# A new hand-laid order for a fused attention and feed-forward kernel: loads, transposes and stores placed anew, batch 2 transposed by DMA, scores by head group

## The chip, the cores and the metric

The kernel runs on one core of a Trainium2 chip. The metric is the time of one execution in microseconds (us). Three executions of the kernel before gave 248.44, 250.93 and 252.87; their median, 250.93 us, is the time before. A further execution was profiled; it took 247.08 us. A change of about 2% is told from no change.

## The reference

The inputs are q, k and v (8 batches, 8 heads, 576 rows, 64 columns) and two weight matrices (512 by 2048 and 2048 by 512). Per batch and head, attention is approximated with 32 landmarks (means of 18 rows):

```
q_lm, k_lm = means of 18 neighbouring rows of q and k          # 32 landmarks
A  = softmax(q    @ k_lm.T / 8)        # 576 x 32
Bm = softmax(q_lm @ k_lm.T / 8)        # 32 x 32
C  = softmax(q_lm @ k.T    / 8)        # 32 x 576
Z  = Bm.T / (norm1(Bm) * norminf(Bm) + 1e-6)
six times:  Z = 2 * Z - Z @ Bm @ Z
x   = A @ Z @ C @ v, heads side by side: 4608 rows of 512
h   = x @ w_in;  out = (h * sigmoid(h)) @ w_out
```

## The kernel before

**Tiling.** The work runs batch by batch. The 8 heads of a batch are two groups (g = 0, 1) of four heads, each with 32 landmarks, so that 128 partitions hold one group's landmarks. q and k arrive with the landmark block on the partitions (`qk`) and are turned into `qT`, with the head's columns on the partitions. `qk`, `qT` and v have two buffers, used by even and odd batches.

**Two ways to transpose.** For batches under `NTR` (3 before) TensorE transposes q and k by an identity (`tr`, 36 matmuls a batch, L515), and VectorE or ScalarE copies the result out of PSUM (`trc`). For later batches SP issues DMA transposes (`xt`, L539), four a batch: q and k by two groups. In the names `xt10.4` is k (1), group 0, batch 4. The exponentials of C (`ce`) have to be transposed too: by TensorE in batches 0 and 1 (`ctm`, `ctc`), by DMA later (`ct0`, `ct1`, L814).

**Per batch.** `ld1`, `ld0` load k and q, `ldv0` to `ldv2` v. `lra` to `lrd` add up the landmarks on VectorE as a tree (L575); in batches 0 and 1 TensorE does it (`lms`). `ltr`, `lmT` transpose the sums; `sb`, `pb` and the names up to `nsd` are Bm and the six steps for Z, which go back and forth between TensorE and VectorE. `A` and `C` are the scores, `Ax`, `Cx` their exponentials on ScalarE; `S`, `Ln`, `Rs`, `etn` normalise A; `cv` multiplies the transposed C with v; `zt`, then `m` multiplies Z C v into `w_in` (copies `mc`).

**Feed-forward.** `h0` to `h15` and `hx0`, `hx8` multiply the normalised A with `m`; `g`, `gx` apply the activation (ScalarE). `p1` to `p7` are seven half-size products of a Strassen-like scheme for 256 rows (names end in `@5000` plus 100 times the batch plus 0, 20 or 40); `ss` are its sums on VectorE, `c1` to `c22` and `u2` copies and additions from PSUM into `ost` (six buffers). `o0` to `o3` is the plain product for the first 256 rows. Each `os` is four stores of 64 KB from SP (in the last batch single ones from SP and ScalarE).

**What sets the order.** `SEQUENCE` lists all steps by name; each engine executes its own in this order, and a queue (SP's, POOL's) issues its DMAs in it. `*n` are n matmuls on zeros that fill TensorE's time. After a slash stands the engine where there is a choice. The list also sets which PSUM bank a step gets. Dependencies in the step objects (`deps`) are asserted against the list; those that concern data become waits, others were rules for the planner that made the list. One kind becomes waits of its own (`o.after`): a transpose `xt` or `ct` waits for the second v load, as it stands in the program, and a load waits for a transpose, so that the two kinds of transfer alternate:

```
            gate = v_ops[b][-2:-1]                    # before an xt of batch b
        gate = last[b - 1].get("xts", [])[-2:-1]      # before the loads of batch b
        if b - 2 >= NCT:
            gate = gate + last[b - 2]["cts"][:1]
```

The order of the two in `xts` is that of the program (k group 0, k group 1, q group 0, q group 1), not that of the list. ScalarE has two sets of tables, for exp/ln and for the activation; each change between them is a table load.

## Time and profile before

| | |
|---|---|
| profiled execution | 247.08 us, its span 245.4 us, granted clock 0.985 in the mean |
| runs of the kernel | 248.44, 250.93, 252.87 us |
| TensorE busy | 233.3 us, 2948 matmuls |
| VectorE, ScalarE busy | 180.0 us, 180.8 us |
| DMA queues | loads (POOL) 18.06 MB; SP's queue 17.35 MB |
| transposes of q and k by DMA | 20, issue to landing 4.2 us in the median |
| transposes of `ce` by DMA | 12, 3.9 us |
| table loads on ScalarE | 12, 1.28 us each |

The page gives busy time by engine, then the span in 40 slices: each digit is a busy share in tenths, and PEclk the clock that TensorE was granted. A windows line has, for a stretch, its length, the busy time of TensorE, its weight loads, VectorE, ScalarE and POOL (instructions in brackets), the granted clock, the DMA share and GB/s. A line of the waits says who waited for whom, the total, the number and the longest. In the chain of work that ended last, the first number is the start and the second the duration.

### The profile page before, as it was taken

The page shows a single profiled execution, that of the slowest core. Times are in us where ns is not written, and L with a number is a line of the kernel's source. Part 1 is how long each engine was busy: PE and PEld are TensorE (multiplying, and loading weights), DVE is VectorE, ACT ScalarE, POOL GpSimd, SP SyncE. Part 2 cuts the span into 40 slices and gives each one's busy share as a digit, 9 for nine tenths or more (in the row PEclk, how much of TensorE's full clock was granted, in tenths as well). Part 3 has the DMA queues.
Part 4 walks back from the last instruction along what each step waited for, and adds up shares of the span by engine and source line. Part 5 has one row for each costly group of instructions (what it writes and reads, how often), then busy time and mean ns, then how long its engine had stood idle before and what let it go on. Part 6 is the DMA issues. An engine that isn't in the chain of part 4 may idle for free.

```text
span 245.4 us, 7471 instructions
## 1 busy us (share of the span) xinstructions
PE 233.3 (95%) x2948; PEld 165.8 (68%) x2948; DVE 180.0 (73%) x503; ACT 180.8 (74%) x432; POOL 36.7 (15%) x62
## 2 busy tenths in 40 slices
PE   7999999999999999199999999999999999999992
PEld 5986464457867556067878754777876765789882
DVE  2589889789998591489798968938899475348752
ACT  3299999988989998159746699999779788634100
POOL 8346713000050040000130060000000000000000
PEclk9999999999999999769999999999999999999999
DMA  6999999999999999793999999985414421012343
GB/s 160 207 203 197 206 207 206 210 205 204 132 177 220 202 137 178 185 194 98 136 190 171 167 185 239 190 145 136 108 47 117 121 52 39 1 43 77 88 119 109
DMA packets 55876, 36.84 MB, mean 150 GB/s; under 512 B 36640, under 2 KB 47392, under 8 KB 55840
## 3 DMA queue, kind: packets, MB, share of 16 engines
q0 software_dynamic: 15120, 18.06, 45.1%
q1 hardware_dynamic: 39808, 17.35, 34.9%
q10 hardware_dynamic: 912, 0.95, 1.4%
q8 instruction: 23, 0.38, 0.6%
q14 instruction: 13, 0.11, 0.1%
HBM read 36.70 MB, written 9.44 MB: 188 GB/s over the span
## 4 chain that ended last, share of the span: by engine, by line
PE 78%; ACT 7%; DMA 7%; SPq 3%; issue 1%; DVE 1%; ACTq 0%; DVEq 0%
PE ps L325 74%; DMA qT<-qk 6%; PE ps L515 3%; SPq L539 2%; ACT gm L913 2%; DMA gm<-in_k_dram 1%; ACT L913 1%; SPq L814 1%; ACT L1116 1%; ACT gx L936 1%; ACT m L335 1%; PE ps L802 1%; DVE red L575 1%; ACT pb L641 1%; ACT et L742 0%
## 5 line engine op out<-in xcount | busy, mean ns | idle before, releaser
L913 ACT ACTIVATE gm<-ps 128x512 f16<-128x512 f32 x128 | 68.7, 621 | 15.0 <-PE ps L325 14.3
L325 PE MATMUL ps<-etn,m 128*128 128x512 bf16 (+1 forms) x512 | 73.5, 289 | 0.2
L325 PEld LDWEIGHTS <-gm 128*128 128x128 f16 x512 | 48.6, 98 | 12.5 <-issue 1.3
L325 PE MATMUL ps<-w_out_sb,gm 128*128 128x256 f16 (+1 forms) x392 | 53.0, 281 | 0.0
L325 PEld LDWEIGHTS <-ss 128*128 128x128 f16 x408 | 39.5, 99 | 9.8 <-issue 1.8
L325 PEld LDWEIGHTS <-m 128*128 128x128 bf16 x512 | 31.5, 98 | 20.8 <-issue 3.2
L325 PE MATMUL ps<-wt,ss 128*128 128x256 f16 x272 | 35.5, 276 | 0.2
L1036 DVE TENSOR_TENSOR ost<-ost,ps 128x256 f32<-128x256 f32 x51 | 20.9, 416 | 13.4 <-PE ps L325 7.4
L335 ACT COPY ost<-ps 128x256 f32<-128x256 f32 (+1 forms) x45 | 17.2, 388 | 10.9 <-PE ps L325 10.6
L335 ACT CAST m<-ps 128x512 bf16<-128x512 f32 x36 | 19.4, 612 | 1.1 <-PE ps L325 0.8
L337 DVE CAST m<-ps 128x512 bf16<-128x512 f32 x28 | 18.3, 685 | 2.3 <-PE ps L325 1.9
L710 DVE SCALAR_TENSOR_TENSOR st<-st,ps 128x128 bf16<-128x128 bf16 (+2 forms) x54 | 13.6, 257 | 8.5 <-PE ps L325 5.5
L407 POOL DMA_DIRECT2D v<-in_v_dram x24 | 14.0, 590 | 30.8 <-DMA qT<-qk 13.6
L325 PE MATMUL ps<-w_out_sb,ss 128*128 128x256 f16 x136 | 17.5, 273 | 0.0
L325 PE MATMUL ps<-wt,gm 128*128 128x256 f16 x120 | 15.5, 272 | 0.0
L575 DVE TENSOR_TENSOR red<-qT 128x1024 f16<-128x1024 bf16 x12 | 8.3, 689 | 9.4 <-DMA qT<-qk 9.2
L685 DVE TENSOR_TENSOR fb<-st,hmask 128x256 bf16<-128x256 bf16 (+1 forms) x54 | 14.4, 271 | 0.8
L752 ACT ACTIVATE ln<-ps 128x288 f32<-128x288 f32 x32 | 12.4, 423 | 2.7 <-PE ps L325 2.4
L787 ACT ACTIVATE ce<-ps 128x288 bf16<-128x288 f32 x32 | 13.0, 424 | 1.7 <-PE ps L325 1.6
L1001 DVE TENSOR_TENSOR ss<-gm 128x1024 f16<-128x1024 f16 x15 | 10.2, 686 | 5.2 <-ACT gm L913 5.2
L742 ACT ACTIVATE et<-ps 128x288 bf16<-128x288 f32 x32 | 11.1, 423 | 3.6 <-PE ps L325 3.6
L337 DVE COPY ost<-ps 128x256 f32<-128x256 f32 x25 | 10.5, 420 | 3.2 <-PE ps L325 3.0
(93 smaller groups left out, 332.0 us busy)
## 6 DMA issues: line engine op xcount, KB each, us to landing
out_dram<-ost SPq DMA_DIRECT2D x126, 64.0 KB, 2.1
v<-in_v_dram POOLq DMA_DIRECT2D x24, 192.0 KB, 10.0
qk<-in_q_dram POOLq DMA_DIRECT2D x7, 576.0 KB, 10.6
qk<-in_k_dram POOLq DMA_DIRECT2D x7, 576.0 KB, 9.2
w_out_sb<-in_moe_w_out_dram POOLq DMA_DIRECT2D x4, 512.0 KB, 15.1
w_in_sb<-in_moe_w_in_dram POOLq DMA_DIRECT2D x8, 128.0 KB, 7.2
w_in_sb<-in_moe_w_in_dram POOLq DMA_DIRECT2D x4, 256.0 KB, 9.0
out_dram<-ost ACTq DMA_DIRECT2D x10, 64.0 KB, 1.7
```

The source lines that it names most:

```text
L325: nc.tensor.matmul(out=out_ap, lhsT=lhsT, rhs=rhs, start=start, stop=stop, skip_group_check=True)
L335: nc.scalar.copy(out=out, in_=in_)
L337: nc.vector.tensor_copy(out=out, in_=in_)
L407: lambda e, a=a: nc.gpsimd.dma_start(out=v_r[b % 2][a * L:(a + 1) * L, :, :], in_=v[b].rearrange("h (l a x) d -> a l h (x d)", l=L, a=VA)[ ...
L575: lambda e: nc.vector.tensor_tensor(out=o_, in0=a_, in1=b_, op=OP.add),
L685: nc.vector.tensor_tensor(out=fb[it % 2][:, g0:g1], in0=bc(sr[it % 3][:, g0:g1, 0:L], 4, 2), in1=bc(hmask, n, 1), op=OP.mult), [o], 14.5 + ...
L710: nc.vector.scalar_tensor_tensor(out=s2[:, g0:g1, lo:SW], in0=s[:, g0:g1, lo:SW], scalar=2.0, in1=ps[:, 0:NG * SW].rearrange("p (g x) -> p ...
L742: lambda e, g=g, et=et, c=c: nc.scalar.activation(out=et[:, c], in_=bank(me["A"], 2 * g + c)[:, 0:HS], func=AF.Exp, scale=sc / J),
L752: lambda e, g=g, c=c, ln=ln: nc.scalar.activation(out=ln[:, c], in_=bank(me["S", g, c])[:, 0:HS], func=AF.Ln),
L787: nc.scalar.activation(out=ce[:, :, 0:VP].rearrange("p (i c) (a l) -> p c a i l", c=2, a=VA)[:, c], in_=bank(me["C"], 2 * g + c)[:, 0:HS]. ...
L913: lambda e, dc=dc, cell=cell: nc.scalar.activation(out=gm[:, dc, :], in_=bank(cell["o"]), func=AF.Silu),
L1036: nc.vector.tensor_tensor(out=out_, in0=x, in1=y, op=OP.add)
```

## The change

- `SEQUENCE` is laid out anew from first step to last: other places on every engine, other engines for some copies (the copies `c` are 33 on ScalarE for 31, `mc` 40 for 36), 67 filler matmuls for 64, 14 table loads for 12.
- `NTR` is 2: batch 2 is transposed by DMA; 36 matmuls and 8 copies go, four DMA transposes come.
- The two groups of k, and of q, are one step (`xt1`, `xt0`), issued one behind the other; the step that others wait for is the first of its two transposes. k always comes first, so the loads of the next batch wait for the first half of q.
- `A` and `C` are two steps each, one by head group, with two PSUM banks a step for four at once.
- Rules of the planner alone go: eight loads in flight at most (`swdge`), A and C after the landmarks' exponentials, the first activation after batch 1's exponentials, most sums of `w_out` after the plain product.

The code, cut:

```diff
-    NTR = 3
+    NTR = 2
...
-        d = list(deps) + list(after)
-        if len(swdge) >= 8:
-            d.append((swdge[-8], None))
+        d = list(deps) + [(x, 0.8) if x.name[:2] == "xt" else x for x in after]
...
-                dep = [a] + plain
+                dep = [a] + (plain if i == 2 else [])
...
-                for g in range(NG):
-                    qt_ops[t, g] = [A(
-                        f"xt{t}{g}.{b}", [("SP", 1.38)],
-                        lambda e, t=t, g=g: nc.sync.dma_start_transpose(
-                            out=qT[:, t, g], in_=qk[:, t, g].rearrange("p j d -> p (j d)")),
-                        [qk_ops[b, t, g]] + use + gate, p0 + 5, lag=XLAG)]
-                    qt_ops[t, g][0].after = gate
-                    me["qk_read"] += qt_ops[t, g]
-                    me["xts"] += qt_ops[t, g]
+                o = A(f"xt{t}.{b}", [("SP", 2.76)],
+                      lambda e, t=t: [nc.sync.dma_start_transpose(
+                          out=qT[:, t, g], in_=qk[:, t, g].rearrange("p j d -> p (j d)"))
+                          for g in range(NG)][0],
+                      [qk_ops[b, t, g] for g in range(NG)] + use + gate, p0 + 5, lag=XLAG)
+                o.after = gate
+                qt_ops[t, 0] = qt_ops[t, 1] = [o]
+                me["qk_read"].append(o)
+                me["xts"] = [o]
...
-        def am(e):
-            for g in range(NG):
+        for g in range(NG):
+            def am(e, g=g):
...
-        me["A"] = A(f"A.{b}", [("PE", 0.26)], am,
-                    lmT_all + ([] if cr else [(pb_op, -0.2)]) + qt_ops[0, 0] + qt_ops[0, 1] + ready, p0 + 20,
-                    psum=4, tiled="q")
+            me["A", g] = A(f"A{g}.{b}", [("PE", 0.142)], am,
+                           lmT_all + qt_ops[0, g], p0 + 20,
+                           psum=2, tiled="q")
...
-        gate = last[b - 1].get("xts", [])[-2:-1]
+        gate = last[b - 1].get("xts", [])
```

The order of the list around the transposes that the prediction speaks of, before (batch 4's transposes, batch 5's loads) and after:

```diff
-nsd40.3 ct0.3 xt00.4 ld1.5 ldv0.4 h9.2 g9.2 g14.2 h1.2 h0.2 g1.2 g0.2 cv0.3 ldv1.5 fb50.3
-ss30@5120.0 ns50.3 wc.3 nsd50.3 zbd.3 ld0.5 h11.2 g11.2 h13.2 g4.2 g13.2 h3.2 g3.2 etn1.3 zt.3
...
-g11.3 p1@5200.0 g3.3 h8.3 g8.3 ss00@5200.0 p5@5200.0 hx0.3 g14.3 g9.3 ss00@5220.0 xt11.4 xt01.4
-xt10.4 ss10@5200.0 lra1.4 lrb1.4 lrc1.4 ss10@5220.0 ss20@5220.0 lrd1.4 lra0.4 lrb0.4 os@5020.0
-ss20@5200.0 l1done.2 ltr1.4 h1.3 h0.3 g0.3 g1.3 g12.3 h15.3 gx0.3 c1@5200.0/DVE p6@5200.0
...
+sb.3 p1@5220.0 l1done.2 gx0.2 ss00@5220.0 gx8.2 xt1.4 C0.3 ss00@5200.0 A1.3 pb.3 p5@5220.0
+ss10@5220.0 ss10@5200.0 p4@5120.0 ss20@5220.0 Cx01.3 p1@5200.0 c1@5220.0/ACT pbs.3 xt0.4 Ax11.3
...
+ct0.3 lra1.4 c5@5220.0/ACT ns00.3 S10.3 p7@5220.0 Ax00.3 Ln10.3 nsd00.3 Cx10.3 fb10.3 os@5021.0
+lrb1.4 S01.3 ns10.3 S00.3 p3@5220.0 Ln01.3 nsd10.3 lrc1.4 Ln00.3 fb20.3 c22@5220.0 Rs0.3 ns20.3
+p5@5200.0 nsd20.3 lrd1.4 ct1.3 ld1.5 fb30.3 lra0.4 ltr1.4 S11.3 ns30.3 p4@5220.0 lmT1.4/ACT ld0.5
...
+fb50.3 cv0.3 wrc.3 Ax11.4 ss30@5200.0 p2@5200.0 Cx01.4 ldv0.5 wc.3 Ax10.4 Cx00.4 ldv1.5 etn0.3
...
+g1.4 ns00.5 h8.4 xt0.6 g10.4 nsd00.5 p2@5300.0 fb10.5 g14.4 ss20@5340.0 g2.4 h15.4 c1@5340.0/DVE
+g8.4 ns10.5 h13.4 nsd10.5 h5.4 fb20.5 g13.4 ss30@5340.0 p6@5340.0 ct1.5 g15.4 lra1.6 h11.4 ld1.7
```

For batches 0 to 2 the loads stand in the new list in this order from the weights on: `wi` pieces and batch 0's v, batch 1's v, `wo0` to `wo2`, `ld1.2`, `ld0.2`, `ldv0.2`, `ldv1.2`, `wo3`, `ldv2.2`; those of batch 3 come after batch 2's transposes on SP and, in SP's queue, eight stores (`os@5000`, `os@5001`), `xt1.3`, `ct0.2`, `ct1.2`, `xt0.3` follow.

## Prediction

> **What bounds the kernel now.** I read the first two parts of the page, then the windows around the one hole in TensorE's row, then who waited for whom, then the queues that feed it.

> ```profile
> span 245.4 us, 7471 instructions
> PE 233.3 (95%) x2948; PEld 165.8 (68%) x2948; DVE 180.0 (73%) x503; ACT 180.8 (74%) x432; POOL 36.7 (15%) x62
> PE   7999999999999999199999999999999999999992
> ...
> PEclk9999999999999999769999999999999999999999
> DMA  6999999999999999793999999985414421012343
> ```

> TensorE is the bound, with one hole, in slice 17. The same stretch in windows, the wait, and the chain:

> ```profile
> 95.00:100.00 5.00, 3.75 (x40) 2.66 (x37) 0.00 (x0) 4.19 (x9) 0.00 (x0) 1.00 1.18 200
> 100.00:105.00 5.00, 0.83 (x3) 0.43 (x4) 3.63 (x8) 0.00 (x0) 0.00 (x0) 0.65 0.70 180
> 105.00:110.00 5.00, 5.00 (x27) 3.11 (x26) 3.95 (x11) 2.75 (x7) 0.00 (x0) 0.66 1.03 197
> ```
> ```profile
> PE ps L325 <- DVE rs L575: 5.4, 1, 5.4
> ```
> ```profile
> 86.72 14.41 DMA qT<-qk
> ...
> 101.23 0.70 DVE red L575
> ```

> TensorE stands 5.4 us for the landmark sums of batch 4 (`ltr1.4`); VectorE could not add because half of k's transpose (`xt10.4`, issued 86.72) took 14.4 us. Then the granted clock is 0.65 and 0.66 in two windows: half speed from 101.5 to 108.4. Work resumed at 104.2, so 4.2 us at half speed lose 2.1 us more. The hole costs 7.5 us. Why 14.4:

> ```profile
> 86.34 0.71 POOL L400 DMA_DIRECT2D qk<-in_k_dram  x1 [13.68 <-issue]
> 87.04 1.16 POOL L407 DMA_DIRECT2D v<-in_v_dram  x2
> 88.20 0.71 POOL L400 DMA_DIRECT2D qk<-in_q_dram  x1
> ```
> ```profile
> DMA to landing us min/median/max: 3.3/4.2/14.4
> ```
> ```profile
> DMA to landing us min/median/max: 2.5/3.9/8.1
> ```

> (The last two: transposes of q and k; of `ce`.) The loads of batch 5 wait for one transpose, `xt00.4`, which stood first; the other three were still to come. In the trace's DMA packets (256 bytes are a transpose's, 768 to 2304 a load's) these loads run from 88.2 to 100.5, and `xt10.4`'s 1152 packets, 1.45 us when alone, run from 89.2 to 100.6: about 100 a us, 41 a us beside 2304-byte packets. `ct0.5` did the same (issued 129.3, first packet 133.4, when the 2304-byte load before it had landed). So: **a transpose that meets a load stream lands with its end.**

> To compare orders I lay TensorE's steps end to end at their undisturbed pitch (start to next start, 20th percentile by kind: `h` 0.43, `p` 0.87, `hx` 0.47, `A` or `C` 0.37, four or five transposes 0.22 or 0.28, filler 0.11). Before has 219.5 us of such work. The real start of a step minus its place in this sum is the delay so far: 4.0 at `sb.0`, 7.5 at `sb.2`, 9.4 just before the hole, 17.0 after it, 21.2 at the end.

> **The change, part by part.** The sum is made against the profiled execution's 247.08 us, its span and 1.68 around it; the median of the runs shown, 250.93, is 1.56% above, and the sum is scaled by that at the end. About 2% is what a measurement of this kernel can tell from no change.

> 1. TensorE loses batch 2's 36 transposes (nine take 0.50 us in the chain): -2.0. Three more fillers: +0.3. **-1.7**.
> 2. A and C in halves: the same 256 matmuls, each half 0.185 by the 0.37 of the whole. **0**; if each of 16 more borders cost 0.1, +1.6.
> 3. The hole: both halves of k and then of q now go out in one order, and the next loads wait for q's first half (and for a `ct` of two batches back). q's second half is issued 1.4 us behind; a load's first packet comes 1.4 to 2.4 us after its issue, so it is gone by then. **-7.5**.
> 4. VectorE loses batch 2's copies out of PSUM (7 at 0.42 to 0.49, about 3.2 us, near 37 us) and gets its tree of sums 9 us later. VectorE is 4.2 to 4.8 busy of 5 there, and the delay grows from 4.0 to 7.5 between 12 and 45 us. **-1.0**; between 0 and -3.4.
> 5. ScalarE has 14 table loads for 12, 1.28 us each; it is 74% busy and steps between holes. **0**; up to +2.6 if both land ahead of a waited-for copy.
> 6. Batch 2's transposes on SP. Up to `ldv2.2` the queue now loads 9.2 MB; before it moved 10.6 MB from 3.7 to 57.8 us (0.196 MB/us), so `ldv1.2`, for which `xt1.2` waits, lands near 47, and the rest (`wo3`, `ldv2.2`) at 50.8. Then four transposes at 1.45: last at 56, sums done at 57.7. `ltr0.2` stands at 50.1 of work, with the delay of 7.5 at 57.6. Nearly hidden, as are `o3` and `wt01`, which need `wo3`: **+0.5** (0 to 2). Queued behind on SP are eight stores of `os@5000` and `os@5001`; six `ost` buffers cover them.
> 7. Batch 3's loads now wait for batch 2's transposes: issue 54, first packet 56, then 1.57 MB with 0.52 MB of stores at 0.22 MB/us (205 to 241 GB/s in the windows from 70 to 80): `xt1.3` at 65.5. `ct0.2` and `ct1.2` are queued behind it, 2.8 and 1.25 us of issue, then 2.5: 72. TensorE is at `cv0.2` at 62.9 + 7.7 = 70.6, and `p4@5100` and all after it wait. **+1.4** (0 to 2.5).
> 8. Batch 4's loads, 1.57 MB and 1.05 MB of stores, end near 87.7; `xt1.4`'s second half lands near 92, 1.5 late for `lra1.4`, some of it covered before `ltr1.4`. **+1.0** (0 to 2.5).
> 9. The new meeting. On SP stand `ct0.3`, four stores, `ct1.3`. `ld1.5` waits for `ct0.3` only. Count from `ct0.3`'s issue: its landing at 2.5, `ld1.5` issued, first packet near 4.5 (4.0 to 5.0); SP issues 1.3 for `ct0.3`, 1.9 for the stores, 1.2 for `ct1.3`: first packet at 4.5 as well, and it needs 0.9 more. `ld1.5` and `ld0.5` are 1.18 MB, 6.0 us at 0.196; the v loads behind them wait for `cv0.3` itself. So `ct1.3` lands at 11.0. Between `ct0.3` and `cv0.3` TensorE has 6.7 us of work (6 `p`, 5 `ns`, 4 `S`, halves of A and C, three small ones). It stands 4.3 us, with no independent step behind. Like the first hole it then loses half of some 4 us: **+4.3 + 2.0**. Bounds: nothing, if the loads' first packet comes at 5.4 or later; 7.5 + 2.5, if the stream is as slow as 1.57 MB in 12.2 us was beside `xt10.4`.
> 10. `ct1.5` goes out just behind `xt0.6`, whose first half lets `ld1.7` go: its packets run from 4.3 to 5.2 us after `xt0.6`'s issue, the loads' from 4.7 to 5.7. **+0.5**.
> 11. The end: as before a last product, a copy and stores in two queues (4.4 us after the last matmul). **0**.

> On the 2.0 of step 9: the trace has one case, half clock from 2.8 us after TensorE stopped. [...]

> Sum: -1.7 - 7.5 - 1.0 + 0.5 + 1.4 + 1.0 + 6.3 + 0.5 = **-0.5**: 246.6 us, and 250.4 by the median. One hole goes and another comes.

> **The rivals.**

> *`ct1.3` escapes.* If the queues shared evenly, 0.9 us of packets would take 1.8 and land near 6.9, when TensorE is there anyway; so too if the loads start 0.9 us later. The sum loses 6.3: 240.3, or **244.0**. For it: starts of loads vary by 1 us, and `ct1.4` of before, 1.8 us ahead of a load's issue, landed in 3.8. Against: `xt10.4` at 41 packets a us, `ct0.5` at none. [...]

> *Both meetings cost, at the slow stream's price: slower.* The place is `ct1.5` before `cv0.5`, 7.5 us of work after `xt0.6`. Starved, it lands at 5.0 + 6.0 + 0.5 = 11.5: 4.0, and 2.0 of clock, for the 0.5: 252.1. If the streams take 9.2 us for 6.0 (that of the 12.2 us above), 3.2 more at each: 258.5. The middle, 255.3, is **259**. It decides from a load's first packet under 5.0 us after `xt0.6`'s issue. For it: six more microseconds of transposes and slower loads in mid-kernel. Against: the margin is 0.5 us in favour, and a first hole gives the queue time.

> *The change doesn't do what it says:* batch 2's transposes starve behind `wo3` and later loads, so that what TensorE saves returns as waits: 2 to 4 us more in steps 6 to 8: **253**. Against: those loads end at 50.8 and the next wait for `xt0.2`.

> **How the numbers follow.** Forecast 0.42 (own range 247 to 254); escape 0.33; two meetings 0.18; batch 2 late 0.07. Of the escape 0.28 lies below 245.9 (-2%); the forecast gives 0.05 there, 0.33 together. Above 255.9 (+2%) lie 0.15 of two meetings, 0.05 of the forecast at its slow price, 0.02 of batch 2: 0.22. The rest, 0.45, is within. The range reaches past the escape by the bound of step 4, to 241, and to 259, where two meetings centre.

> **What would show it.** Right: no wait for `rs` of 5 us near 98; a transpose of `ce` that takes over 8 us from issue to landing near 100; TensorE waiting for `ct` 4 us there, with a granted clock under 0.8 in one slice; TensorE's transposes of q and k at 72 matmuls for 108. The escape: all transposes of `ce` under 6 us and PEclk at 9 throughout. Wrong altogether: a hole before 50 us, which no step has, or one after 160, where loads have ended.

## The result, and the profile after

The changed kernel is slower by 6.2%: 262.49 us in the median of four runs (261.86 to 263.48) against 249.69 of the kernel before (245.99 to 252.87); ratio 1.062, 95% interval 1.052 to 1.073. Ratios leave out executions that lie over 1.5% above the fastest of their kernel, here two of the kernel before; the medians alone give 1.051. The forecast was 250.4, its range 241 to 259. Below, spans of profiled executions are compared: 260.5 for 245.4 us. The four runs of the changed kernel lie within 1.6 us, so smaller differences between single profiles are not read. Those of the kernel before lie within 6.9 us, and its profile, from an execution of 247.08, is one of the short ones. Where no view is quoted, a transfer lands with its last DMA packet; the views count to the signal that a waiting engine sees, 0.4 to 2.6 us later for the changed kernel's transposes. The page after:

```profile
span 260.5 us, 7370 instructions
PE 238.9 (92%) x2915; PEld 166.3 (64%) x2915; DVE 175.7 (67%) x491; ACT 186.9 (72%) x438; POOL 36.8 (14%) x62
PE   8999999999949999379989995999999999999993
...
PEclk9999999999976999958999998899999999999999
DMA  6999999999699999967989969999533013033044
```

One hole has become three (the 12th, the 17th and 18th, and the 25th slice), each with a dip of PEclk beside it. DMA stays at 6 or more to the end of slice 28, 182 us; in the kernel before, slice 19 apart, to the end of slice 27, 166 us. TensorE's waits, then windows at the first two places:

```profile
PE ps L324 <- DMA ct<-ce: 5.3, 3, 3.6
PE ps L324 <- ACT lmT L334: 4.5, 1, 4.5
PE ps L324 <- DVE st L707: 2.9, 1, 2.9
```
```profile
70.00:75.00 5.00, 3.03 (x44) 2.49 (x42) 3.36 (x13) 3.64 (x6) 0.00 (x0) 1.00 0.75 109
75.00:80.00 5.00, 3.09 (x60) 2.28 (x61) 2.02 (x4) 0.00 (x1) 0.00 (x0) 0.54 1.18 179
...
105.00:110.00 5.00, 1.19 (x13) 0.82 (x10) 2.38 (x8) 0.22 (x2) 0.37 (x1) 0.95 1.01 179
110.00:115.00 5.00, 2.94 (x72) 1.72 (x73) 0.93 (x2) 2.98 (x12) 0.66 (x2) 0.50 0.64 122
115.00:120.00 5.00, 5.00 (x53) 3.02 (x51) 2.61 (x12) 2.61 (x8) 1.06 (x2) 0.52 0.86 121
```

With the prediction's own measure, a step's start minus its place in TensorE's undisturbed work:

| step | before | after |
|---|---|---|
| `sb.2` | 7.5 | 9.6 |
| `m0.2` | 8.3 | 16.8 |
| `ns30.3` | 8.6 | 18.5 |
| `m0.3` | 9.1 | 28.5 |
| `cv0.5` | 18.3 | 34.0 |
| `m0.5` | 18.9 | 36.0 |
| end | 21.2 | 37.9 |

The end is 16.7 later, less 1.6 of work saved (219.5 to 217.9): the 15.1 of the spans. The three places:

- **Near 73 to 84 us** (6.9 more delay): `cv0.2` waits 3.6 us for `ct0.2` and `ct1.2`; the clock is half from 75.4 to 82.2.
- **Near 105 to 120** (9.9): `sb.4` waits 4.5 for `lmT0.4`, a copy on ScalarE; then `cv0.3`'s second half waits 1.4 for `ct1.3`; the clock is half from 109.5 to 119.8.
- **Near 157 to 165** (5.1): `A1.5` waits 2.9 for VectorE; the clock is half from 160.7 to 164.1.

Who held ScalarE and VectorE there, from the order of time:

```profile
109.98 0.37 ACT L334 COPY ost<-ps 128x256 f32<-128x256 f32 x1 [4.78 <-DMA out_dram<-ost]
...
159.55 0.69 DVE L572 TENSOR_TENSOR red<-qT 128x1024 f16<-128x1024 bf16 x1 [4.01 <-DMA qT<-qk]
```

ScalarE's copy `c5@5200.0`, ahead of `lmT0.4`, waited for an `ost` buffer whose store, issued at 104.8 beside `ld1.5`, signalled its landing at 109.9; VectorE's `lra0.6` waited for `xt0.6`, with the steps of Z behind it. Each wait ends at a DMA. The two queues, SP's and then POOL's (idle before the instruction in brackets):

```profile
48.83 6.19 SPq L534 DMA_TRANSPOSE qT<-qk  x4
55.14 6.63 SPq L975 DMA_DIRECT2D out_dram<-ost  x8
70.54 2.75 SPq L534 DMA_TRANSPOSE qT<-qk  x2
73.40 2.58 SPq L811 DMA_TRANSPOSE ct<-ce  x2
76.07 2.75 SPq L534 DMA_TRANSPOSE qT<-qk  x2
78.92 12.88 SPq L975 DMA_DIRECT2D out_dram<-ost  x16
94.06 6.38 SPq L534 DMA_TRANSPOSE qT<-qk  x4
100.54 1.28 SPq L811 DMA_TRANSPOSE ct<-ce  x1
```
```profile
56.23 0.71 POOL L397 DMA_DIRECT2D qk<-in_k_dram  x1 [19.48 <-DMA qT<-qk]
...
81.79 0.71 POOL L397 DMA_DIRECT2D qk<-in_k_dram  x1 [22.42 <-DMA qT<-qk]
...
103.80 0.71 POOL L397 DMA_DIRECT2D qk<-in_k_dram  x1 [18.87 <-DMA ct<-ce]
```

This is a loop: batch 3's loads (56.2) wait for batch 2's transposes (48.8 to 55), `xt1.3` (70.5) for those loads, `ct` stands behind it and `xt0.3` behind `ct`, batch 4's loads (81.8) wait for `xt0.3`, `xt1.4` (94.1) for those, and so on to `ld1.7` at 158.6. Not every gate in it is a DMA: in the turn from 103.8 to 134.1 the v loads of batch 5 waited 9.0 us for TensorE (`cv0.3`, which reads the v buffer), and `xt1.5` went at 124.9, 6.0 after its v load had signalled, behind `ct0.4` and `ct1.4`.

### The profile page after: what moved, and what is told of

Read it like the earlier page. It is cut to its first block, busy times and chain, and to the rows that moved or that the text cites. A ratio compares the mean times of both kernels' runs of the same rounds, so it can differ in the third digit from the quotient of the medians.

```text
span 260.5 us, 7370 instructions
## 1 busy us (share of the span) xinstructions
PE 238.9 (92%) x2915; PEld 166.3 (64%) x2915; DVE 175.7 (67%) x491; ACT 186.9 (72%) x438; POOL 36.8 (14%) x62
## 5 line engine op out<-in xcount | busy, mean ns | idle before, releaser
L910 ACT ACTIVATE gm<-ps 128x512 f16<-128x512 f32 x128 | 67.2, 632 | 7.4 <-PE ps L324 7.3
L324 PE MATMUL ps<-etn,m 128*128 128x512 bf16 (+1 forms) x512 | 70.3, 286 | 0.0
L324 PE MATMUL ps<-w_out_sb,gm 128*128 128x256 f16 (+1 forms) x392 | 55.2, 287 | 0.3 <-ACT pb L638 0.3
L334 ACT COPY ost<-ps 128x256 f32<-128x256 f32 (+1 forms) x47 | 17.8, 387 | 21.6 <-DMA out_dram<-ost 12.5
L334 ACT CAST m<-ps 128x512 bf16<-128x512 f32 x40 | 22.0, 595 | 7.3 <-PE ps L324 7.2
L707 DVE SCALAR_TENSOR_TENSOR st<-st,ps 128x128 bf16<-128x128 bf16 (+2 forms) x54 | 14.0, 261 | 15.4 <-PE ps L324 12.7
L336 DVE CAST m<-ps 128x512 bf16<-128x512 f32 x24 | 15.9, 686 | 4.9 <-PE ps L324 4.9
L397 POOL DMA_DIRECT2D qk<-in_k_dram x7 | 5.0, 711 | 100.3 <-DMA qT<-qk 81.3
L324 PE MATMUL ps<-w_out_sb,ss 128*128 128x256 f16 x136 | 19.1, 290 | 0.0
L336 DVE COPY ost<-ps 128x256 f32<-128x256 f32 (+1 forms) x23 | 9.8, 432 | 10.2 <-PE ps L324 8.4
L324 PEld LDWEIGHTS <-fb 128*128 128x128 bf16 x96 | 8.2, 99 | 8.9 <-DVE fb L682 3.7
L739 ACT ACTIVATE et<-ps 128x288 bf16<-128x288 f32 x32 | 12.4, 418 | 1.8 <-PE ps L324 1.7
## 6 DMA issues: line engine op xcount, KB each, us to landing
qk<-in_q_dram POOLq DMA_DIRECT2D x7, 576.0 KB, 10.6
```

The lines of the kernel that those rows point to most:

```text
L324: nc.tensor.matmul(out=out_ap, lhsT=lhsT, rhs=rhs, start=start, stop=stop, skip_group_check=True)
L334: nc.scalar.copy(out=out, in_=in_)
L336: nc.vector.tensor_copy(out=out, in_=in_)
L397: lambda e, t=t, src=src: nc.gpsimd.dma_start(out=qk_r[b % 2][:, t].rearrange("p g j d -> p g (j d)"), in_=src[b].rearrange("(g h) (l j) d ...
L707: nc.vector.scalar_tensor_tensor(out=s2[:, g0:g1, lo:SW], in0=s[:, g0:g1, lo:SW], scalar=2.0, in1=ps[:, 0:NG * SW].rearrange("p (g x) -> p ...
L739: lambda e, g=g, et=et, c=c: nc.scalar.activation(out=et[:, c], in_=bank(me["A", g], c)[:, 0:HS], func=AF.Exp, scale=sc / J),
```

## Experiments: the waits where TensorE shows them

The first theory was four local causes, one edit each.

**e1_load_waits**
```diff
-            gate = gate + last[b - 2]["cts"][:1]
+            gate = gate + last[b - 2]["cts"][:2 if b == 5 else 1]
```

> The loads of batch 5 wait for both transposes of ce two batches back instead of the first; all else as in the changed kernel (span 260.5). Theory: ct1.3 and the last stores of os@5021.0 are both late because they meet this load stream. Then ct1.3 lands under 4 us after its issue, ScalarE's wait of 4.8 us for a store near 110 falls under 2.5, TensorE's lag between 100 and 120 us grows by about 2 instead of 9.9, and the span is about 252.5. Rival 1: the stores are slow of themselves; ScalarE still waits 4 us or more, sb.4 stays near 110.7, and the span is about 257.5. Rival 2: the loads, some 4 us later, make batch 5's transposes late, and a new hole near 125 to 135 takes back more than half: 256 to 258.

Span 258.6. The mechanism was right: `ct1.3` landed 2.0 us after its issue, ScalarE's wait fell to 1.4, and the delay at `m0.3` was 20.3 instead of 28.5. But 8 us came back between `m0.3` and `m0.4` (28.7 there, 30.7 in the changed kernel): TensorE now stood 2.8 us for `ct0.4`, and half clock followed. This is rival 2.

**e2_lmT_first**
```diff
-p7@5200.0 c5@5200.0/ACT lmT0.4/ACT
+p7@5200.0 lmT0.4/ACT c5@5200.0/ACT
```

> On ScalarE the copy lmT0.4 goes ahead of c5@5200.0, the copy that waits 4.8 us for a buffer of ost; nothing else changes. Theory: the buffer's wait and the starved ct1.3 lie in one hole, and ct1.3 (landing near 113) ends it, so sb.4, C0.4 and A1.4 move ahead by some 4 us, TensorE's wait for ct grows from 1.4 to about 4 to 5, cv0.3's second half stays near 113, and the span falls by about 1 (259 to 260). Rival: the buffer's wait sets the loss by itself; then the span falls by 4.5 and the half clock behind it, to 253 to 255.

`sb.4` came at 105.2 instead of 110.7, TensorE's longest wait for `ct` became 6.7, and `m0.3` still had a delay of 27.6: the two waits share one hole, and `ct1.3` ends it. So there is no gain. The span is 263.1; 1.9 us of that lie behind `p1@5700.0`, where nothing was changed, and are not explained.

**e3_ct_ahead**
```diff
-S11.2 xt1.3 f0.2 ... ct0.2 ... ct1.2 ns30.2
+S11.2 f0.2 ... ct0.2 ... ct1.2 xt1.3 ns30.2
```

> In SP's queue ct0.2 and ct1.2 go ahead of xt1.3. Theory: the 3.6 us wait of TensorE at 76.6 is the sum of batch 3's late loads and of xt1.3's 2.8 us of issue ahead of the two; they still wait for the loads (ldv1.3), so they go at 70.5, ct1.2 lands near 74.2, TensorE stands about 1 us, too short for half clock: lag from 70 to 85 us grows by 1.5 instead of 7, span about 255. xt1.3 is 2.6 us later and nothing waits for it. Rival: the place in the queue is worth nothing because xt1.3's transposes are then late for lra1.3 and C0.3; a hole of 2 to 3 us near 85 to 95 comes instead and the span stays at 258 to 261.

The first hole went whole: delay 11.1 at `sb.3` for 17.0. At `ns30.3` it was 18.9 for 18.5, and the span 260.1. What took it back:

```profile
98.39 0.69 DVE L572 TENSOR_TENSOR red<-qT 128x1024 f16<-128x1024 bf16 x1 [4.16 <-DMA qT<-qk]
```

TensorE came 6 us earlier to a place that needs `xt1.4`, and `xt1.4` went at 93.6 as against 94.1.

**e4_lra_later**
```diff
-xt0.6 ... lra0.6 ... lrb0.6 ... lrc0.6 ... Ax11.5 lrd0.6
+xt0.6 ... Ax11.5 lra0.6 lrb0.6 lrc0.6 lrd0.6
```

> On VectorE the first three of batch 6's sums for q (lra0.6, lrb0.6, lrc0.6) stand later in the order, just ahead of lrd0.6; the transposes stay as they are. Theory: the hole at 157.6 to 160.5 is VectorE waiting 4.0 us in its order for xt0.6's second half (landed 158.84), with the steps of Z that TensorE needs queued behind it; so the hole of 2.9 and the half clock after it go, 4 to 5 us, and the span is about 256. Rival: TensorE then waits at the same place for something else (A's banks, ct1.5, the table load on ScalarE at 158), and the span is 259 to 260.5.

Span 260.9: `A1.5` no longer waits, and TensorE stands 2.6 us for `ct1.5` one step on, then for the sums (1.0) and a bank (1.4). This is the rival.

**e5_all**: the four edits together.

> The four edits so far in one kernel: batch 5's loads wait for both transposes of ce, lmT0.4 ahead of c5@5200.0, ct0.2 and ct1.2 ahead of xt1.3, batch 6's sums for q later on VectorE. Theory 1 (what is left of the step by step picture): each hole had its own cause, and each edit alone was only cancelled by the next hole in line, so together they bring most of 7 + 10 + 4.5 us: span 242 to 247. Theory 2: from 50 to 175 us the time is set by one chain of DMAs, in which loads wait for the transposes of the batch before and transposes for the loads; the edits don't shorten it (the second lengthens it), only the last holes move: xt1.4 goes at 93 to 95 as in all five kernels, ld1.6 at 130 to 133, and the span is 255 to 260.

Span 258.1, `xt1.4` at 94.4, `ld1.6` at 131.6: all three are theory 2's. The four holes were where the DMA side showed, not what made the time.

## Experiments: the loop of loads and transposes

**e8_half_loads**
```diff
-out=qk_r[b % 2][:, t].rearrange(...), in_=src[b].rearrange(...)
+out=qk_r[b % 2][:, t, 0:NG if b < 3 else 1].rearrange(...),
+in_=src[b].rearrange(...)[:, 0:NG if b < 3 else 1]
```

> The changed kernel with the k and q loads of batches 3 to 7 cut to their first four heads: 0.59 MB less a batch, everything else (transposes, matmuls) as before, so the output of the other heads is not the reference's. Chain theory: every batch's turn of loads is 3 us shorter, xt1.3 goes at 67, xt1.4 at 88, ld1.6 near 123, xt1.7 near 158 instead of 173; the holes of TensorE shrink to a few us in sum and the span is 244 to 250. Rival, holes made by the order of steps beside them: ct1.3 lands earlier and gains 3 us, the other holes stay, 254 to 258.

```profile
span 246.2 us, 7365 instructions
...
PE   8899999999989999699699999999999999999990
...
PEclk9999999999999999999999999999999999999996
```

This is 14.3 us less for five turns of 3.0: nearly all of it reached the end, and the clock stayed up until the end. No matmul was taken away.

**e11_fewer_xt**
```diff
-                          for g in range(NG)][0],
+                          for g in range(NG if t or b < 3 else 1)][0],
```

> The changed kernel without the second transpose of q (group 1) in batches 3 to 7: five DMA transposes of 1.4 us less; the heads of group 1 use old q, so their output is not the reference's. Loop theory: transposes and loads take turns, so each turn is 1.4 us shorter just as e8's was 3, and the span falls by 5 to 7: 253.5 to 255.5; ld1.6 goes near 129 instead of 134. Rival: the loop's length is the loads' alone, because the next loads wait only for q's first half: 259 to 260.5.

Span 256.1, 4.4 less; `ld1.6` at 131.0. Transposes count too, a little less than the 5 to 7 expected.

**e9_before_half**: the cut of e8_half_loads in the kernel before.

> The kernel before with the same cut of loads as e8_half_loads (k and q of batches 3 to 7 for the first four heads only, the other heads' output not the reference's). In the changed kernel this cut took 14 of 260 us. Theory: only the changed order puts the loop of loads and transposes on the path that sets the end; the kernel before meets its loads in one place alone (the hole near 100), so no more than that hole, 5 to 8 us, can go: span 238 to 241. Rival: the loop binds the kernel before as well, and the cut takes 10 us or more: 235 or less.

```profile
span 240.5 us, 7471 instructions
...
PE   7989999999999999799999999999999999999992
...
PEclk9999999999999999999999999999999999999999
```

Span 240.5, 4.9 less, and PEclk at 9 in every slice. The delay at `sb.4`, behind the old hole, is 12.0 for 17.0, and the difference stays there to the end: the old hole and no more. Against the median of eleven executions of the kernel before taken beside it (250.23; 247.84 to 252.51), its own 242.23 is 8.0 less. **So the same cut is worth 14.3 in the changed order and 5 to 8 in the old one:** the rest, 6 to 9 us of loop, came onto the path with the change.

## Experiments: which part of the change

**e7_pe_batch2**
```diff
-    NTR = 2
+    NTR = 3
...
-xt1.2 ... xt0.2
+tr15.2 ... trc15.2/DVE ... tr05.2 ... trc05.2/DVE
```

> The changed kernel with batch 2 transposed by TensorE again: 36 matmuls in eight steps with eight copies (seven on VectorE, one on ScalarE) between 32 and 45 us, no xt1.2 and xt0.2, and so no wait of batch 3's loads for them; all else in the changed order. Chain theory: batch 3's loads follow the others without a break and are done by 62 instead of 71, the hole before cv0.2 (7 us with its clock) goes, ld1.4 goes 5 to 6 us earlier, xt1.4 at 87 to 90 instead of 94, and the later holes shrink too; against 2 us of transposes: span 247 to 253. Rival: only the hole before cv0.2 goes and the others stay, because they are made by the order near them: 255 to 257. Rival 2: VectorE's copies near 37 to 45 us cost what they save: 258 or more.

Span 260.9, not the 247 to 253 of the theory. Batch 3's loads had landed by 60.5 instead of 71, as expected, and it was worth nothing. This is what stands ahead in SP's queue:

```profile
60.30 5.81 SPq L975 DMA_DIRECT2D out_dram<-ost  x8
66.28 3.21 SPq L534 DMA_TRANSPOSE qT<-qk  x2
72.89 2.54 SPq L811 DMA_TRANSPOSE ct<-ce  x2
75.53 2.87 SPq L534 DMA_TRANSPOSE qT<-qk  x2
```

**e13_free_queue** has these transposes of TensorE later in the list, by up to 2.6 us of its time (it had waited 1.6 us for `ld1.2` there; now 0.8), and adds:
```diff
-os@5000.0 ... ldv2.3 ... os@5001.0 ... xt1.3 ... ct0.2 ... ct1.2 ... xt0.3
+ldv2.3 xt1.3 xt0.3 os@5000.0 ... os@5001.0 ... ct0.2 ... ct1.2
```

> e7_pe_batch2 with its two flaws mended: TensorE's transposes of batch 2 stand 2 to 3 us later (there it stood 1.8 us for ld1.2), and in SP's queue xt1.3 and xt0.3 go ahead of the stores os@5000.0 and os@5001.0 and of ct0.2, ct1.2 (there batch 3's loads had landed by 60.5, but xt1.3 went only at 66.3 and xt0.3 at 75.5, behind these). Loop theory: xt1.3 goes near 59, xt0.3 near 62, batch 4's loads wait for ct0.2 alone and go at 74 to 76 instead of 82, xt1.4 near 88 instead of 94, span 253 to 256. If the loop is entered earlier and the span still stays at 258 or more, the loop is held by TensorE's own order (ct waits for C's exponentials) and not by the queue.

```profile
59.60 5.71 SPq L534 DMA_TRANSPOSE qT<-qk  x4
65.36 4.49 SPq L975 DMA_DIRECT2D out_dram<-ost  x8
72.86 2.54 SPq L811 DMA_TRANSPOSE ct<-ce  x2
```

Span 251.5; batch 4's loads go at 75.9, and TensorE's delay at `m0.3` is 16.3 for 28.5.

**e15_queue_only**: the queue edit without the other.

> The changed kernel (batch 2 by DMA) with only the queue edit of e13_free_queue: xt1.3 and xt0.3 ahead of os@5000.0, os@5001.0, ct0.2 and ct1.2. Spans so far: neither edit 260.5, batch 2 by TensorE alone 260.9, both 251.5. If batch 2's transposes matter through the loop, batch 3's loads still end near 70, xt1.3 goes at 68 to 70, ct1.2 lands near 79 instead of 77, and this edit alone gains nothing: span 259 to 263 (both parts are needed for the 9 us). If the queue's order alone is the cause: 251 to 254.

```profile
PE ps L324 <- ACT ost L334: 11.3, 1, 11.3
```

Span 267.8, worse than either expectation: with batch 2's transposes in the way batch 3's loads end at 68.2, `xt1.3` goes at 67.6, and the eight stores now queued behind it keep the `ost` buffers full, so that ScalarE and then TensorE stand. Together:

| span | old place in SP's queue | `xt.3` ahead |
|---|---|---|
| batch 2 by DMA | 260.5 | 267.8 |
| batch 2 by TensorE | 260.9 | 251.5 |

Neither part alone gains; the two together are worth 9 us, in one profile each. What the later place of TensorE's transposes adds in the last cell was not tried alone.

**e14_all_again**: e13_free_queue with e1's, e2's and e4's edits.

> e13_free_queue with three of the local edits: batch 5's loads wait for both ct of batch 3, lmT0.4 ahead of c5@5200.0, batch 6's sums for q later on VectorE. Loop theory: where the loop leaves room, the local holes near 106 to 118 and 158 are real and their edits now count: 3 to 8 us below e13_free_queue, 246 to 252. Rival: no more than 2 us below e13_free_queue, as with e5_all.

Span 254.8, 3.3 more, which neither expectation had. e1's edit sends batch 5's loads 1.9 us later (103.2), and `ld1.7` goes 2.0 later. In this one profile the loop still weighs more than the local holes.

**e12_early_loads**
```diff
-                me["xts"] = [o]
+                me["xts"] = me["xts"] or [o]
```

> The changed kernel with the next loads waiting for k's transposes (issued first) instead of q's (and for ct as before). Loop theory: batch 3's loads go near 53.5 instead of 56.2, batch 4's near 77 instead of 82, batch 6's near 129 instead of 134, and the span falls by 4 to 6, to 254.5 to 256.5. Rival: q's transposes then meet the loads and land with their end, as xt10.4 did in the kernel before; TensorE stands for A instead, and the span is 259 or more.

Span 281.9: this is the rival, and far worse than it said. The transposes into `qT`, from issue to landing (3.2/3.7/5.7 in the changed kernel):

```profile
DMA to landing us min/median/max: 3.2/3.5/15.3
```

In the DMA packets the second halves of q of batches 2, 3 and 5 land 13.4, 13.9 and 14.7 us after their issue, against 2.9 to 4.7 in the changed kernel. The two queues' packets went about one for one: from 89 to 97 us of this run 1001 packets of loads (2304, then 768 bytes) and 1041 of transposes (256 bytes) began. In the kernel before, too, 1005 and 1060 began from 89 to 100 us, during `xt10.4`. Equal shares of the time, as in the prediction's escape, do not agree with this: `xt10.4`'s packets, 1.45 us when alone, would have taken 2.9 and took 11.4. One batch's loads are 1280 packets in the trace and one transpose into `qT` is 1152: so one that met the start of a stream landed near its end (`xt10.4` at 100.6, the loads at 100.5).

## Experiments: the old hole

**e6_before_fixed**, the kernel before:
```diff
-ct0.3 xt00.4 ld1.5 ... xt11.4 xt01.4 xt10.4
+ct0.3 xt10.4 xt11.4 xt01.4 xt00.4 ld1.5
```

> The kernel before with one edit: xt10.4, xt11.4, xt01.4 and xt00.4 go out in this order ahead of ld1.5, so that the loads of batch 5 wait for the last of the four instead of the first. The prediction's step 3 says 7.5 us: no wait for rs near 98, clock 1.0 throughout, span 238, ratio to before 0.97. If the DMA chain has no slack in the kernel before either, the 4 us by which batch 5's loads go later come back as a wait near 115 to 135, and the ratio is 0.98 to 1.0.

Ratio 0.995 (0.988 to 1.001): no change that can be told. In the profile the delay at `sb.4` fell from 17.0 to 10.0, the 7.0 of the hole; 5.4 came back by `cv0.4` (15.4), half of it this:

```profile
DVE red L575 <- DMA qT<-qk: 3.4, 1, 3.4
PE ps L325 <- DVE ost L1036: 3.0, 1, 3.0
```

Batch 5's sums stood first on VectorE, their transposes came later than TensorE's now earlier work, and a sum into `ost` that TensorE needed stood behind them.

**e10_before_two** adds:
```diff
-lra1.5 lrb1.5 lrc1.5 p7@5200.0 c22@5200.0 lrd1.5 ... c5@5220.0/DVE
+p7@5200.0 c22@5200.0 ... c5@5220.0/DVE lra1.5 lrb1.5 lrc1.5 lrd1.5
```

> The kernel before with two edits: that of e6_before_fixed, and batch 5's sums for k (lra1.5 to lrd1.5) later on VectorE, behind c5@5220.0, since in e6_before_fixed VectorE stood 3.4 us at lra1.5 for the transposes of batch 5, and the sums into ost that TensorE needed a bank from stood behind it. Theory: the wait of 3.0 us at 108 and its half clock go, 4 to 5 us, and nothing else moves: span 238 to 240, ratio 0.97 to 0.98. Rival: the loads, 6 us later than in the kernel before, then show in the next step that needs batch 5 (ltr1.5, cv0.4): span 241 to 244, ratio 0.985 to 1.0.

Ratio 0.980 (0.973 to 0.987), 245.19 us in the median of six: probably faster than both kernels, but at the edge of the 2% that can be told and of the theory's 0.97 to 0.98. Its one profile, from an execution of 246.24, has a span of 244.5, which is nearer the rival's: there the delay at `cv0.4` is 13.4, 2.0 less than in e6_before_fixed, and the gain is given back by `cv0.6`, with three waits for `ct` of 2.3 us in sum.

## The prediction, step by step

- **Step 1**: right. 72 transposes for 108, TensorE's work 1.6 less. Step 11 was right too (4.5 us after the last matmul for 4.4). Steps 2 and 5 were not tried alone.
- **Step 3**: the hole went, as worked out, and no `xt` took over 5.7 us. Its size was that of the place: the profile of e6_before_fixed shows 7.0 there and 2.3 at the end, and its ten executions no clear gain. This was the largest term, and in that profile its net was a third of what it stood for.
- **Step 4**: wrong sign. The delay at 43 us is 9.3 for 7.4. VectorE was relieved (15.47 busy for 18.15 from 20 to 40 us), but the delay did not fall with it.
- **Step 6**: right; batch 2's transposes landed at 56.5 for 56.
- **Step 7**: mis-sized. `ct1.2` landed at 76.9 for 72. The loads were issued at 56.2 for 54, and `xt1.3` followed 14.3 us behind them; the step had 11.5. From 68.5 to 71 the packets show 8 to 13 of 768 bytes per half microsecond where 120 went before: a tail that a mean rate of 0.22 MB/us hides. The term was 1.4 and measured 6.9, its clock included.
- **Step 8**: mis-sized for the same reason: `xt1.4`'s second half landed at 98.9 for 92. It cost 1.7 for 1.0 there, since TensorE was late by then.
- **Step 9**: the meeting was right nearly to the microsecond (first packet of `ld1.5` 4.7 after `ct0.3`'s issue for 4.5; `ct1.3` landed 12.5 after it for 11.0). It missed that the last stores of `os@5021.0`, ahead of `ct1.3` in SP's queue, meet the same loads, and that ScalarE and `sb.4` hang on them: `ct1.3`'s own first packet came at 9.0 for 4.5 and went one for one with the loads' (154 for 162 from 110 to 112 us). TensorE stood 4.5 for `lmT0.4` and only 1.4 for `ct1.3`, where 4.3 for `ct` was forecast, and the place cost 9.9 for 6.3.
- **Step 10**: `ct1.5` escaped, as said (2.2 us). The hole came all the same, from `lra0.6` on VectorE, which no step had: 5.1. So the second rival's 259 came near the time, but its mechanism, a starved `ct1.5`, did not come.

The sum was -0.5 and the spans differ by +15.1. Of these 15.6 us, steps 7 and 9 were 5.5 and 3.6 too small, and 5.1 had no step. Terms too small are one part of the error. The other is that they were added as if each lateness ended where it showed. In the second rival the prediction says that "a first hole gives the queue time". e3_ct_ahead and e5_all show the opposite: a hole gives the queue little, because the queue is what is late. In all seventeen profiled kernels but e12_early_loads, the kernel before among them, 101 to 105 us pass from the issue of `ld1.7` to the end of the span: 102.5 before, 101.9 after, 104.7 with half loads. The question to ask was when `ld1.7` goes. One turn from loads to loads took 22 to 30 us, the four turns from `ld1.3` to `ld1.7` 102.4. Between the same two places of the list TensorE has 76.3 us of undisturbed work, 18 to 20 a turn. The difference is 26, and by 24 its delay grew (9.6 at `sb.2`, 33.9 at `A1.5`): it could stand early or late, but stand it had to. In the kernel before `ld1.3` went at 31.6, without a wait for batch 2, so that the same loop began 25 us earlier. Of these 25 us 14.9 are left when `ld1.4` goes (66.9 before, 81.8 after), and they are the whole loss: from there to the end the two profiles have 178.5 and 178.7 us, though TensorE by then has 8 us less work left in the changed kernel.

So the step that failed is step 7, the turn of batch 3: its loads wait for batch 2's transposes, and `xt0.3`, which the next loads wait for, stands behind `ct0.2` and `ct1.2`. It was priced at +1.4, as a lateness that ends at `cv0.2`. It measured 6.9 there, and it made every later turn late: undoing both of its parts (e13_free_queue) took 9.0 of the 15.1 us back, where mending the four places where it showed (e5_all) took 2.4.

What stays open: which gaps made step 4's 2 us, what makes the slow tail of the loads, why e11_fewer_xt gave less than it took away, and how far e13_free_queue's remaining 6 us over the kernel before are the loop's.

## What to carry to other kernels

Where loads wait for transposes and transposes for loads, lay the loop out first: one turn's loads, its tail, each issue in the queue ahead of the next gate; compare the turn with the compute that the order has between one gate and the next, and follow it to the last load. If it is the longer one, a wait seen on an engine is where the loop shows, and mending it moves the wait: cutting one member of the loop in a test kernel tells this in one run, and the same cut in the kernel before tells whether the change put the loop there. A step taken off an engine and put on a queue that is already in such a loop is not free, however idle the queue looks in the mean (here 34.9% of the DMA engines' time in the kernel before).

## What the hardware showed that was not expected

A hole of TensorE can be over before the clock falls for it. In the changed kernel TensorE stopped at 157.6 and worked again from 160.5:

```profile
159.00:160.00 1.00, 0.00 (x0) 0.00 (x0) 0.45 (x1) 0.74 (x2) 1.00 (x2) 1.00 0.71 157
160.00:161.00 1.00, 0.51 (x29) 0.37 (x31) 0.97 (x4) 0.12 (x1) 0.01 (x1) 0.87 0.82 48
161.00:162.00 1.00, 0.87 (x48) 0.65 (x37) 1.00 (x4) 0.59 (x2) 0.11 (x1) 0.50 0.96 207
...
164.00:165.00 1.00, 1.00 (x10) 0.86 (x9) 0.88 (x3) 0.00 (x0) 0.00 (x0) 0.92 1.10 243
```

The granted clock (the column after POOL's) halves from 160.7 to 164.1, after the work had resumed. In e11_fewer_xt a hole of 2.3 us was followed by half clock from 156.8 to 160.2 in the same way. These holes of 2.3 and 2.9 us thus cost half of 3.4, about 1.7 us, more. But in e4_lra_later a hole of 2.6 us, from 156.8 to 159.3, cost nothing more:

```profile
155.00:160.00 5.00, 2.41 (x78) 1.50 (x76) 1.59 (x5) 4.02 (x8) 1.41 (x2) 1.00 0.96 165
160.00:165.00 5.00, 4.04 (x38) 3.45 (x37) 4.19 (x12) 1.88 (x7) 1.73 (x3) 1.00 1.04 203
```
